# Top-k attention and a leaky-ReLU MLP on one core: the order on ScalarE, scores a slot earlier, a smaller first chunk of tokens and other operations for rounding weights

## The chip, the cores and the metric

The kernel runs on one NeuronCore of a Trainium2 chip. The core has TensorE (PE, matmuls; PEld is its loading of weights), VectorE (DVE), ScalarE (ACT), GpSimd (POOL) and SyncE (SP, which issues the DMAs here). Each has its own instruction queue and works through it in order; semaphores tie them together. The metric is the device time of one execution in microseconds, lower is better.

## What is computed

Attention over 8 batches of 8 heads, 576 tokens and 64 dimensions, in which each query keeps its 32 highest scores, and a two-layer MLP with leaky ReLU on the 4608 tokens of 512 features that come out. All in float32; the MLP's weights arrive as 64-bit floats.

```python
scores = scale * np.matmul(q, k.transpose(0, 1, 3, 2))
kth = np.partition(scores, -top_k, axis=-1)[..., -top_k:-top_k + 1]   # top_k = 32
scores = np.where(scores >= kth, scores, -1000000000.0)
attn = np.exp(scores - np.max(scores, axis=-1, keepdims=True))
attn = attn / (np.sum(attn, axis=-1, keepdims=True) + 1e-09)
x = np.matmul(attn, v)            # then (B,H,S,D) -> (B*S, H*D)
h = x @ w_in                      # 512 -> 2048
out = np.maximum(0.01 * h, h) @ w_out
```

## The kernel before

Heads go in pairs, so that two heads fill 128 partitions of q and k; four pairs make a batch. A *unit* is 128 queries of one pair ("whole") or 64 queries of two pairs ("left", since 576 = 4 x 128 + 64). There are 18 units per batch, 144 in all. A unit is two score tiles of 128 x 576, `u.s[0]` and `u.s[1]`.

The main loop (`for s in ...`, 147 *slots*) is a pipeline written out by hand under `tc.manual_schedule()`: each engine's order is the order of the calls in the loop. In slot s the unit `cur` (s) has its top-k on DVE (`top_k`, L183 and L186: four rounds of two MAX8, three of them with two MATCH_REPLACE8), the unit `old` (s-1) is masked on POOL (`mask`, L195 to L199), `older` (s-2) gets its exponents on ScalarE (`exponents`, L202), its sum plus 1e-9 on POOL (`sums`, L207) and the reciprocal on DVE (`reciprocals`, L211), and `oldest` (s-3, `LAG`) is normalized on ScalarE (`normalize`, L214), transposed on PE with evictions on ScalarE (`transpose_main`, L221 and L223, twice; `transpose_tail`, L228 and L229) and multiplied with the values (`weigh_values`, L251, eviction into the MLP's input `x`, L261). Scores for `new` (s+1) are made on PE and evicted by ScalarE (`scores`, L164 and L173).

The MLP is cut into token chunks, `CHUNKS`. A chunk is ready three slots after its last unit; `slot_budget` spreads its work evenly over the slots until the next chunk is ready, and `mlp_steps` issues that much at each of six places (`SLOTS`) in a slot. A step is two matmuls, of the first pass (L271, tile `ph`, eviction with leaky ReLU L277 into `gT`) or of the second (L282, tile `pz`, eviction L289, store L290). `mlp_cost` counts the work in columns. [...]

In the first slots the weights are turned from 64-bit into 32-bit floats, 32 chunks of 128 x 512 (`convert_weights`, L104 to L114): DVE takes exponent and mantissa bits (L104, L105), POOL clamps the exponent (L106), ScalarE scales both (L107, L108), and in the next call of `convert`, DVE puts them together (L110, L112) and POOL multiplies (L114). Each raw chunk has one of three buffers, and its load (L93) waits for one; a slot calls `convert` three or four times.

## Time and profile before

| | |
|---|---|
| median of 3 runs | 1966.16 us (1962.93 to 1968.38) |
| the profiled execution's own time | 1969.71 us |
| its span, first to last instruction | 1967.9 us |
| PE busy | 1651.5 us, 84% |
| DVE busy | 1498.1 us, 76% |
| POOL busy | 1189.6 us, 60% |
| ScalarE busy | 987.9 us, 50% |

The profile is of one execution. A busy share is the time in which an engine works on some instruction; PE's matmuls overlap and their ends are modelled. An average over the span mixes stages with different limits, so stretches and single slots are read as well. A wait is put down to the instruction that released it.

### The profile page before, as it was taken

Reading aid. Unit: us, or ns where it says so; the run is one execution under the profiler, and the core shown is the slowest. Engines: PE = TensorE matmul, PEld = TensorE weight load, DVE = VectorE, ACT = ScalarE, POOL = GpSimd, SP = SyncE. Lnnn points to the kernel's source line nnn. Section 1 sums busy time; section 2 is a strip of 40 time slices with the busy share of each in tenths; the row PEclk is TensorE's granted clock in tenths of the full one; section 3 lists DMA queues with packets and bytes.
Section 4 is the critical chain, followed back from the end, with each engine's and each line's share of the span. In section 5 each row is a group of like instructions: output and inputs, shape, how many; then the busy total and the mean of one; then the engine's idle time right before and its main releaser. Section 6 shows DMA issues by size and latency. Waiting matters only on the chain.

```text
span 1967.9 us, 25462 instructions
## 1 busy us (share of the span) xinstructions
PE 1651.5 (84%) x8864; PEld 963.6 (49%) x8864; DVE 1498.1 (76%) x3152; ACT 987.9 (50%) x2069; POOL 1189.6 (60%) x934
## 2 busy tenths in 40 slices
PE   2124688889899899898898898898898999899999
PEld 1123556455455455455455455455455455455575
DVE  7888988888887877777787877887787777776700
ACT  2344555565555555555555555555555455555441
POOL 5766766666665666666666665665665666665520
PEclk9956899999999999999999999999999999999999
DMA  4232010001100010000100010000100010000000
GB/s 163 80 110 87 12 54 13 18 6 37 36 18 1 11 54 19 18 6 25 38 28 1 11 54 13 18 12 25 36 30 1 6 36 8 11 11 1 12 6 16
DMA packets 22976, 56.22 MB, mean 29 GB/s; under 512 B 2240, under 2 KB 2240, under 8 KB 22848
## 3 DMA queue, kind: packets, MB, share of 16 engines
q1 hardware_dynamic: 22848, 54.60, 8.3%
q8 instruction: 70, 1.15, 0.2%
q14 instruction: 58, 0.48, 0.1%
HBM read 45.15 MB, written 9.44 MB: 28 GB/s over the span
## 4 chain that ended last, share of the span: by engine, by line
PE 71%; ACT 18%; POOL 4%; issue 3%; DVE 2%; DMA 0%; SPq 0%; POOLq 0%; ACTq 0%
PE pz L282 25%; PE ph L271 18%; PE psc L164 9%; PE po L251 9%; PE main L221 8%; ACT s_sb L214 7%; ACT s_sb L202 4%; ACT wT L223 4%; PE tail L228 2%; ACT s_sb L173 2%; ACT gT L277 1%; POOL pen L197 1%; POOL w_in L114 1%; POOL ex L106 1%; POOL w_out L114 1%
## 5 line engine op out<-in xcount | busy, mean ns | idle before, releaser
L197 POOL TENSOR_SCALAR pen<-s_sb,tops 128x576 f32<-128x576 f32 x288 | 639.5, 2221 | 27.3
L183 DVE MAX8 tops<-rest 128x8 f32<-128x576 f32 x864 | 607.7, 744 | 0.0
L271 PE MATMUL ph<-x,w_in 128*128 128x384 f32 (+2 forms) x1792 | 575.4, 457 | 0.0
L282 PE MATMUL pz<-w_out,gT 128*128 128x512 f32 x1152 | 542.0, 603 | 0.0
L221 PE MATMUL main<-ident,s_sb 128*115 128x128 f32 x1152 | 203.0, 301 | 273.0 <-ACT s_sb L214 271.7
L199 POOL TENSOR_TENSOR s_sb<-s_sb,pen 128x576 f32<-128x576 f32 x288 | 411.9, 1430 | 24.0
L186 DVE MATCH_REPLACE8 rest<-tops,rest 128x576 f32<-128x576 f32 x576 | 423.1, 742 | 0.0
L207 POOL TENSOR_SCALAR ze<-z 128x2 f32<-128x2 f32 x144 | 37.3, 259 | 604.3 <-ACT s_sb L202 604.2
L271 PEld LDWEIGHTS ph<-x,w_in 128*128 128x128 f32 x1792 | 308.1, 196 | 146.9 <-issue 40.4
L221 PEld LDWEIGHTS main<-ident,s_sb 128*115 128x115 f32 x1152 | 156.9, 187 | 399.8 <-ACT s_sb L214 336.0
L211 DVE RECIPROCAL rz<-ze 128x2 f32<-128x2 f32 x144 | 23.7, 165 | 372.8 <-POOL ze L207 372.6
L282 PEld LDWEIGHTS pz<-w_out,gT 128*128 128x128 f32 x1152 | 203.7, 192 | 200.8 <-issue 199.7
L173 ACT COPY s_sb<-psc 128x576 f32<-128x576 f32 x288 | 169.9, 642 | 189.7 <-PE psc L164 189.7
L223 ACT COPY wT<-main 115x512 f32<-115x512 f32 x288 | 168.7, 586 | 156.8 <-PE main L221 155.3
L164 PE MATMUL psc<-kt,qt 64*128 64x288 f32 (+1 forms) x1280 | 203.0, 439 | 38.6 <-ACT s_sb L173 31.2
L214 ACT ACTIVATE s_sb<-s_sb,rz 128x576 f32<-128x576 f32 x288 | 222.9, 774 | 0.0
L202 ACT ACTIVATE s_sb<-s_sb,nbias 128x576 f32<-128x576 f32 x288 | 222.7, 773 | 0.0
L186 DVE MATCH_REPLACE8 rest<-tops,s_sb 128x576 f32<-128x576 f32 x288 | 211.5, 742 | 0.0
L183 DVE MAX8 tops<-s_sb 128x8 f32<-128x576 f32 x288 | 202.0, 742 | 7.3 <-ACT s_sb L173 7.3
L251 PEld LDWEIGHTS po<-wT,vt 115*64 115x64 f32 (+1 forms) x3200 | 162.0, 140 | 88.4 <-issue 82.6
L251 PE MATMUL po<-wT,vt 115*64 115x128 f32 (+3 forms) x3200 | 195.9, 272 | 1.0 <-ACT wT L223 1.0
L164 PEld LDWEIGHTS psc<-kt,qt 64*128 64x128 f32 (+1 forms) x1280 | 110.4, 182 | 108.2 <-issue 45.5
(26 smaller groups left out, 677.9 us busy)
## 6 DMA issues: line engine op xcount, KB each, us to landing
vt<-in_vk_dram SPq DMA_DIRECT2D x32, 290.0 KB
qt<-in_qT_dram SPq DMA_DIRECT2D x32, 288.0 KB
kt<-in_kT_dram SPq DMA_DIRECT2D x32, 288.0 KB
out_dram<-o_sb SPq DMA_DIRECT2D x36, 256.0 KB
raw<-in_moe_w_in_dram SPq DMA_DIRECT2D x16, 512.0 KB
raw<-in_moe_w_out_dram SPq DMA_DIRECT2D x16, 512.0 KB
```

Of the source, the lines that this page charges most:

```text
L164: nc.tensor.matmul(ps[i][r0:r0 + u.rows, half, 0:HS], qt[d, u.q0:u.q0 + u.rows], kt[d, half * HS:(half + 1) * HS], start=True, stop=True,)
L183: nc.vector.max(out=u.tops[:, i, r, :], in_=src[i])
L186: nc.vector.match_replace(out=rest[i], in_to_replace=u.tops[:, i, r, :], in_values=src[i], imm_value=LOWEST)
L197: nc.gpsimd.tensor_scalar(pen, u.s[i], u.tops[:, i, ROUNDS - 1, 7:8], MASKED, ALU.is_lt, ALU.mult)
L199: nc.gpsimd.tensor_tensor(u.s[i], u.s[i], pen, ALU.add)
L202: nc.scalar.activation(u.s[i], u.s[i], AF.Exp, bias=u.nbias[:, i:i + 1], scale=SCALE, accum_out=u.z[:, i:i + 1])
L214: nc.scalar.activation(u.s[i], u.s[i], AF.Copy, bias=0.0, scale=u.rz[:, i:i + 1])
L221: nc.tensor.transpose(main[0:KLEN[c], c, :], u.s[i][:, c * KSTEP:c * KSTEP + KLEN[c]], ident)
L223: nc.scalar.copy(u.wT[0:KSTEP, i, 0:NKC - 1, :], main[0:KSTEP])
L251: nc.tensor.matmul(po[side * D:(side + 1) * D, o, :], vt[0:KLEN[c], c, side, :], u.wT[0:KLEN[c], i, c, r0:r0 + n], start=(c == 0), stop=(c ...
L271: nc.tensor.matmul(ph[:, 0:n], w_in[c][:, f * P:(f + 1) * P], x[c][:, 0:n], start=(c == 0), stop=(c == HP - 1),)
L282: nc.tensor.matmul(pz[:, 0:DMODEL], gT[f][:, i * P:(i + 1) * P], w_out[f // 4][:, f % 4, :], start=(f == 0), stop=(f == NFC - 1),)
```

## The change

On ScalarE both normalizes of `oldest` come first in a slot, and exponents come ahead of the transposes' evictions; the sum plus 1e-9 moves from POOL to ScalarE. Both masks of `old` come first on POOL. `scores` now serves unit s+2 and stands right after `weigh_values`. The MLP is issued at seven places. The chunks of tokens begin with 64 and 128 and end with 192, and in even batches the left units (tokens 0 to 63) come first, in odd ones last. `convert` keeps two chunks in flight and is called four times per slot. The two bit operations on DVE take their constants from a 128 x 1 tile `bits`, read as a repeated column, as second tensor operand; the mantissa and the fraction are kept in the destination instead of a `man` tile and the raw buffer. One value tile, one output tile fewer; q and k are loaded a slot earlier.

The diff, cut to its core (of the loop only what stands there now):

```diff
-    CHUNKS = [128, 256] + [384] * 10 + [256, 128]
+    CHUNKS = [64, 128] + [384] * 11 + [192]
...
-        frac = lo.bitcast(F32)
-        ex = raws.tile([P, WCH], U32, name="ex", bufs=2)
-        man = raws.tile([P, WCH], U32, name="man", bufs=2)
-        nc.vector.tensor_scalar(ex, hi, 20, 0x7FF, ALU.logical_shift_right, ALU.bitwise_and)
-        nc.vector.tensor_scalar(man, hi, 0xFFFFF, None, ALU.bitwise_and)
+        frac, man = lo.bitcast(F32), dst.bitcast(U32)
+        ex = raws.tile([P, WCH], U32, name="ex")
+        nc.vector.scalar_tensor_tensor(out=ex, in0=hi, scalar=20, in1=bits[:, 0:1].to_broadcast([P, WCH]),
+                                       op0=ALU.logical_shift_right, op1=ALU.bitwise_and)
+        nc.vector.tensor_tensor(man, hi, bits[:, 1:2].to_broadcast([P, WCH]), ALU.bitwise_and)
...
-        nc.vector.scalar_tensor_tensor(out=frac, in0=man, scalar=2.0 ** -20, in1=frac,
+        nc.vector.scalar_tensor_tensor(out=dst, in0=man, scalar=2.0 ** -20, in1=frac,
...
-        nc.gpsimd.tensor_tensor(dst, frac, ex.bitcast(F32), ALU.mult)
+        nc.gpsimd.tensor_tensor(dst, dst, ex.bitcast(F32), ALU.mult)
...
+        first = b % 2 == 0
...
-        units += left + whole if b % 2 else whole + left
+        units += left + whole if first else whole + left
...
-        nc.gpsimd.tensor_scalar(u.ze, u.z, 1e-9, None, ALU.add)
+        nc.scalar.activation(u.ze, u.z, AF.Copy, bias=1e-9, scale=1.0)
...
-    SLOTS = 6
+    SLOTS = 7
...
-        finish_conversions()
+        if len(converting) == 2 or not raw_chunks:
+            for c in converting[:1]:
+                next(converting.pop(0), None)
...
             next(picks, None)
             if old:
                 mask(old, 0)
+                mask(old, 1)
+            if oldest:
+                normalize(oldest, 0)
+                normalize(oldest, 1)
+            convert()
+            mlp_steps(budget)
+            if older:
+                exponents(older, 0)
+            if oldest:
+                transpose_main(oldest, 0)
+            mlp_steps(budget)
+            next(picks, None)
+            convert()
+            if older:
+                exponents(older, 1)
+                sums(older)
+            if oldest:
+                transpose_main(oldest, 1)
+            mlp_steps(budget)
+            if oldest:
+                transpose_tail(oldest)
+            next(picks, None)
+            convert()
+            mlp_steps(budget)
+            if older:
+                reciprocals(older)
+            mlp_steps(budget)
+            next(picks, None)
+            if oldest:
+                weigh_values(oldest)
             if new:
                 scores(new)
             convert()
             mlp_steps(budget)
...
             mlp_steps(budget)
             attended(s)
```

How this moves instructions, at three places. ScalarE before, one slot in the middle of the kernel, from the evictions of scores to the eviction of `x` (`s_sb` are score tiles, with numbers; L202 is the exponent, L214 the normalize, L223 and L229 evict transposes):

```order
L173 COPY s_sb_6957<-psc_6951 128x576
L173 COPY s_sb_6959<-psc_6952 128x576
L202 ACTIVATE s_sb_6703,z<-s_sb_6703,nbias 128x576
L214 ACTIVATE s_sb_6615<-s_sb_6615,rz 128x576
L202 ACTIVATE s_sb_6705,z<-s_sb_6705,nbias 128x576
L223 COPY wT<-main 115x512
L214 ACTIVATE s_sb_6617<-s_sb_6617,rz 128x576
L223 COPY wT<-main 115x512
L229 COPY wT<-tail 116x2x128
L289 COPY o_sb<-pz 128x512
L261 COPY x_6054<-po 128x128
```

ScalarE after, a slot of the same kind (L178 evicts scores, L219 normalizes, L207 is the exponent, L212 the sum, L228 and L234 evict transposes):

```order
L178 COPY s_sb_6401<-psc_6395 128x576
L178 COPY s_sb_6403<-psc_6396 128x576
L219 ACTIVATE s_sb_6069<-s_sb_6069,rz 128x576
L219 ACTIVATE s_sb_6071<-s_sb_6071,rz 128x576
L207 ACTIVATE s_sb_6150,z<-s_sb_6150,nbias 128x576
L228 COPY wT<-main 115x512
L207 ACTIVATE s_sb_6152,z<-s_sb_6152,nbias 128x576
L212 ACTIVATE ze<-z 128x2
L228 COPY wT<-main 115x512
L234 COPY wT<-tail 116x2x128
L266 COPY x_5532<-po 128x128
```

The two normalizes moved from behind the exponents, and the second one from behind an eviction of transposes, to right behind the scores' evictions.

PE before, from the transposes of one slot to the scores that stand at the head of the next (L221 and L228 transposes, L282 MLP, L251 values, L164 scores):

```order
L221 MATMUL main<-ident,s_sb_6615 115x128 x4
L221 MATMUL main<-ident,s_sb_6617 115x128 x4
L282 MATMUL pz<-w_out_94,gT_107 128x512
L282 MATMUL pz<-w_out_94,gT_108 128x512
L228 MATMUL tail<-ident,s_sb_6615 116x128
L228 MATMUL tail<-ident,s_sb_6617 116x128
L282 MATMUL pz<-w_out_94,gT_109 128x512
L282 MATMUL pz<-w_out_94,gT_110 128x512
L251 MATMUL po<-wT,vt 64x128 x10
L164 MATMUL psc_7037<-kt,qt 128x288
L164 MATMUL psc_7038<-kt,qt 128x288
L164 MATMUL psc_7037<-kt,qt 128x288
```

PE after, the same piece of a slot (L226 and L233 transposes, L288 MLP, L256 values, L169 scores):

```order
L226 MATMUL main<-ident,s_sb_5986 115x128 x4
L226 MATMUL main<-ident,s_sb_5988 115x128 x4
L288 MATMUL pz<-w_out_94,gT_100 128x512
L288 MATMUL pz<-w_out_94,gT_101 128x512
L233 MATMUL tail<-ident,s_sb_5986 116x128
L233 MATMUL tail<-ident,s_sb_5988 116x128
L288 MATMUL pz<-w_out_95,gT_102 128x512
L288 MATMUL pz<-w_out_95,gT_103 128x512
L256 MATMUL po<-wT,vt 64x128 x10
L169 MATMUL psc_6395<-kt,qt 128x288
L169 MATMUL psc_6396<-kt,qt 128x288
L169 MATMUL psc_6395<-kt,qt 128x288
```

Nothing moved on PE here: the scores stand behind the value products in both, at the end of a slot instead of the head of the next.

DVE before, in the first unit, two calls of `convert` with a round of top-k between them:

```order
L110 SCALAR_TENSOR_TENSOR raw<-man,raw 128x512
L112 SCALAR_TENSOR_TENSOR ex<-raw,ex 128x512
L104 TENSOR_SCALAR ex<-raw 128x512
L105 TENSOR_SCALAR man<-raw 128x512
L183 MAX tops<-rest_156 128x8
L183 MAX tops<-rest_157 128x8
L186 MATCH_REPLACE rest_156<-tops,rest_156 128x576
L186 MATCH_REPLACE rest_157<-tops,rest_157 128x576
L110 SCALAR_TENSOR_TENSOR raw<-man,raw 128x512
L112 SCALAR_TENSOR_TENSOR ex<-raw,ex 128x512
```

DVE after, the calls at the same place:

```order
L114 SCALAR_TENSOR_TENSOR w_in_90<-w_in_90,raw 128x512
L116 SCALAR_TENSOR_TENSOR ex<-raw,ex 128x512
L107 SCALAR_TENSOR_TENSOR ex<-raw,bits 128x512
L109 TENSOR_TENSOR w_in_92<-raw,bits 128x512
L188 MAX tops<-rest_167 128x8
L188 MAX tops<-rest_168 128x8
L114 SCALAR_TENSOR_TENSOR w_in_91<-w_in_91,raw 128x512
L116 SCALAR_TENSOR_TENSOR ex<-raw,ex 128x512
L107 SCALAR_TENSOR_TENSOR ex<-raw,bits 128x512
L109 TENSOR_TENSOR w_in_93<-raw,bits 128x512
```

Each call finishes the chunk that was begun two calls earlier (`w_in_90`, then `w_in_91`) instead of the one before, and L105's tile `man` is gone.

## Rows read from the trace of the kernel before

**Rows 1.** engines' busy time and share of the span, instructions (the page)

```profile
PE 1651.5 (84%) x8864; PEld 963.6 (49%) x8864; DVE 1498.1 (76%) x3152; ACT 987.9 (50%) x2069; POOL 1189.6 (60%) x934
```

**Rows 2.** busy time of each engine (and instructions) in two stretches; then granted clock, DMA share, GB/s

```profile
413.30:1755.50 1342.20, 1214.49 (x6456) 681.39 (x6456) 1059.87 (x2273) 710.74 (x1479) 835.27 (x650) 0.99 0.06 21
1755.50:1967.90 212.40, 208.43 (x1006) 128.17 (x1002) 83.07 (x180) 85.05 (x187) 74.51 (x59) 1.00 0.03 9
```

**Rows 3.** the same view, of the reciprocals L211 alone, in three stretches

```profile
68.60:205.80 137.20, 0.91 (x6) 0.68 0.28 94
219.70:248.80 29.10, 0.44 (x3) 0.97 0.01 1
418.25:1760.70 1342.45, 17.92 (x108) 0.99 0.06 21
```

**Rows 4.** timeline of PE: start, us, what; in brackets idle time before, its releaser

```profile
1100.16 0.69 PE L221 MATMUL main<-ident,s_sb 128*115 128x128 f32 x4 [1.35 <-ACT s_sb L214]
...
1106.86 3.70 PE L282 MATMUL pz<-w_out,gT 128*128 128x512 f32 x8
1110.39 0.60 PE L221 MATMUL main<-ident,s_sb 128*115 128x128 f32 x4
1112.34 0.69 PE L221 MATMUL main<-ident,s_sb 128*115 128x128 f32 x4 [1.35 <-ACT s_sb L214]
```

**Rows 5.** timeline of ScalarE in the same slot

```profile
1107.01 1.18 ACT L173 COPY s_sb<-psc 128x576 f32<-128x576 f32 x2 [0.94 <-PE psc L164]
...
1108.85 0.77 ACT L214 ACTIVATE s_sb<-s_sb,rz 128x576 f32<-128x576 f32 x1
1109.51 0.77 ACT L202 ACTIVATE s_sb<-s_sb,nbias 128x576 f32<-128x576 f32 x1
...
1111.03 0.59 ACT L223 COPY wT<-main 115x512 f32<-115x512 f32 x1 [0.66 <-PE main L221]
1111.51 0.78 ACT L214 ACTIVATE s_sb<-s_sb,rz 128x576 f32<-128x576 f32 x1
```

**Rows 6.** waits, slots 27 to 134: us in total, times, longest

```profile
PE main L221 <- ACT s_sb L214: 126.6, 125, 1.4
```

**Rows 7.** groups by line, the conversion's four on DVE: busy us, mean ns

```profile
L105 DVE TENSOR_SCALAR man<-raw 128x512 uint32<-128x512 uint32 x32 | 33.2, 1037 | 0.0
L110 DVE SCALAR_TENSOR_TENSOR raw<-man,raw 128x512 f32<-128x512 uint32 x32 | 28.7, 898 | 0.1
...
L112 DVE SCALAR_TENSOR_TENSOR ex<-raw,ex 128x512 uint32<-128x512 uint32 x32 | 21.9, 683 | 24.0 <-ACT ex L108 24.0
...
L104 DVE TENSOR_SCALAR ex<-raw 128x512 uint32<-128x512 uint32 x32 | 13.6, 425 | 4.4 <-DMA raw<-in_moe_w_in_dram 4.4
```

**Rows 8.** timeline of DVE and GpSimd, at two places of the conversion

```profile
61.78 1.40 POOL L199 TENSOR_TENSOR s_sb<-s_sb,pen 128x576 f32<-128x576 f32 x1
62.00 1.73 DVE L110 SCALAR_TENSOR_TENSOR raw<-man,raw 128x512 f32<-128x512 uint32 x1
...
98.65 0.41 DVE L104 TENSOR_SCALAR ex<-raw 128x512 uint32<-128x512 uint32 x1
98.80 1.41 POOL L114 TENSOR_TENSOR w_in<-raw,ex 128x512 f32<-128x512 f32 x1 [1.23 <-DVE ex L112]
98.98 1.51 DVE L105 TENSOR_SCALAR man<-raw 128x512 uint32<-128x512 uint32 x1
```

**Rows 9.** timeline of DVE and ScalarE at the start

```profile
7.30 1.42 DVE L183 MAX8 tops<-s_sb 128x8 f32<-128x576 f32 x2 [7.30 <-ACT s_sb L173]
...
11.96 1.18 ACT L173 COPY s_sb<-psc 128x576 f32<-128x576 f32 x2 [4.15 <-PE psc L164]
```

**Rows 10.** weight loads: DMA rate in 4 us; issue on SP; the wait for it

```profile
100.00:104.00 4.00, 0.89 (x4) 0.89 (x4) 4.00 (x9) 3.00 (x7) 0.99 (x3) 0.61 0.35 131
...
22.63 11.21 SPq L93 DMA_DIRECT2D raw<-in_moe_w_in_dram  x3
...
35.37 0.43 DVE L104 TENSOR_SCALAR ex<-raw 128x512 uint32<-128x512 uint32 x1 [4.39 <-DMA raw<-in_moe_w_in_dram]
```

More of the change, by code (lines that the diff above doesn't have):

```diff
@@ L150 @@
     for b in range(B):
[L151 removed]
+        first = b % 2 == 0
+        whole = [Unit(b, [b * HP + hp], q0 + LEFT * first)
                  for q0 in range(0, S - LEFT, P) for hp in range(HP)]
[L153 removed]
+        left = [Unit(b, [b * HP + hp, b * HP + hp + 1], 0 if first else S - LEFT)
                 for hp in range(0, HP, 2)]
[L155 removed]
+        units += left + whole if first else whole + left
     def scores(u):
@@ L278, in mlp @@
             yield 2 * max(n, 225)
-        for i in range(n // P):
+        for r0 in range(0, n, P):
+            m = min(P, n - r0)
             pz = ps_ml.tile([P, 512], F32, name="pz", tag="ml")
@@ L365 @@
         last = {p: n for n, u in enumerate(units) for p in u.pairs}
-        load_qk(0)
-        scores(units[0])
-        fetch_weights()
-        for p in range(1, HP):
+        for p in range(HP):
             load_qk(p)
-            fetch_weights()
-        for p in range(HP):
-            load_v(p)
+            if p % 2:
+                scores(units[p // 2])
+            if p < 3:
+                fetch_weights()
         def load_more(s):
-            for of, load, lag in ((qk_of, load_qk, -1), (v_of, load_v, LAG)):
-                while len(of) < NPAIR and (len(of) < LOADED or last[len(of) - LOADED] + lag <= s):
+            for of, load, n, lag in ((qk_of, load_qk, LOADED, -2), (v_of, load_v, LOADED_V, LAG)):
+                while len(of) < NPAIR and (len(of) < n or last[len(of) - n] + lag <= s):
                     load(len(of))
         for s in range(len(units) + LAG):
-            cur, new, old = unit(s), unit(s + 1), unit(s - 1)
-            older, oldest = unit(s - 2), unit(s - LAG)
+            cur, old = unit(s), unit(s - 1)
+            older, oldest, new = unit(s - 2), unit(s - LAG), unit(s + 2)
             picks = top_k(cur) if cur else iter(())
@@ L389 @@
                 mask(old, 0)
-            if new:
-                scores(new)
+                mask(old, 1)
+            if oldest:
+                normalize(oldest, 0)
+                normalize(oldest, 1)
             convert()
```

45 lines of the change are left out of this document (16 added, 29 removed).

## The prediction, made before the changed kernel ran

> **What bounds the kernel now.** I read the busy shares first [rows 1], then the stretches [rows 2], then the period of the loop, taken from the one reciprocal that each slot issues [rows 3], then one slot on PE and ScalarE [rows 4, 5] and the waits [rows 6]. "Slot" is one pass of the loop over units, s = 0 to 146.
>
> PE is the fullest engine, yet only 84% busy, and VectorE (DVE) comes second with 76% [rows 1]. The shares hide three stages. While weights are converted, six slots took 137.2 us, 22.9 us each; DVE sets that pace. Behind it three slots took 29.1 us, 9.70 each, with DVE still the pace: that is what one slot's top-k costs it. From slot 27 to 134, 108 slots took 1342.4 us, 12.43 each [rows 3]. There DVE is busy for 1059.9 of 1342 us and PE for 1214.5 [rows 2], so neither is full: a wait sets the period. PE's wait for ScalarE's normalize (L214) comes to 126.6 us in that stretch, 1.17 per slot [rows 6]. Rows 4 and 5 show why. In this slot PE runs its MLP steps to 1110.39, then the first transposes; the second ones start only at 1112.34, 1.35 us after PE went idle. On ScalarE the second normalize starts at 1111.51, because ahead of it in the queue stand two score evictions, two exponents and the eviction of the first transposes. DVE's idle 282 us there are the echo: it has nothing to do until the slot moves on. After slot 134 more MLP work is handed to each slot and PE is full (208.4 of 212.4 us [rows 2]).
>
> **The change, part by part.**
>
> *ScalarE's order (slots 21 to 140).* PE's own order in these slots does not change: scores of unit s+2 at the end of slot s are the same place as before at the start of slot s+1. So the gain must come from ScalarE. Now both normalizes stand directly behind the score evictions. From the end of PE's scores: evictions 1.18, two normalizes at about 0.67 from start to start [rows 5] make 2.5 us. PE meanwhile has four MLP matmuls, 3.53 us [rows 4], then the first transposes, so neither pair of transposes waits. In slots of the first MLP pass an MLP eviction (at most the 0.59 us of the eviction in rows 5) can stand ahead, and PE's cover is four to six matmuls of 384 columns, 2.6 to 4 us at 1.72 ns a column (below); it still holds, but by 0.1 or 0.2 us in one slot of three. What is late next: the exponents and then the sum, now on ScalarE (144 instructions on two elements; at a third of a normalize's 0.77 us, an estimate, 37 us on an engine that is 53% busy here [rows 2]). DVE's reciprocal waits for that sum, and behind it stand only the last round of that unit and the next unit. DVE needs 9.70 of a longer slot, and the normalize that needs the reciprocal comes half a slot later. GpSimd loses the sum, and with it a wait on ScalarE in front of its mask; the mask has a slot in hand. So I take the whole wait away: 12.43 - 1.17 = 11.26 us a slot. Bounds: 11.0 (the slot of rows 4, 12.18 from one second transposes to the next, would be 10.83 without the gap), and 11.85 if half of the wait comes back.
>
> *Rounding of weights (slots 0 to 8).* Before, a chunk costs DVE L104, L105, L110, L112: 0.425 + 1.037 + 0.898 + 0.683 = 3.04 us [rows 7], about 2.74 from start to start. Undisturbed they cost 0.33, 0.33, 0.60, 0.60 = 1.86, so 0.88 per chunk is blocking: L105 takes 1.51 when GpSimd's multiply slips in, L110 takes 1.73 beside GpSimd's add [rows 8]. The new L107 and L109 read two operands and can't be faster than L110's 0.60, so the free cost rises to 2.40. Whether they block is not in the trace, since no operand there is a repeated column. Ends: 2.40 (nothing blocks) and 4.55 (each chunk pays both of the worst cases, 1.1 and 1.05). I take 2.40 + 0.88 = 3.28, as L110, the nearest row, is blocked too.
>
> The Trainium skill (SBUF — State Buffer, Who interferes with whom) says that a VectorE instruction with two SBUF inputs contends with a GpSimd instruction that reads SBUF. L110's rows agree; by that rule the new forms escape nothing, and the value near 3.28 or above holds; with forms that escape it the sum would be 28 us lower.
>
> Two chunks are now in flight, so the 24.0 us in which DVE's L112 waited for ScalarE's exponent [rows 7] go; I take 0 left. The raw buffer is now free when DVE has read it, not after GpSimd's multiply, but the load that takes it is needed at the next conversion call instead of the one after. The gap is two of the new operations, a round of top-k and two more: 1.2 + 2.8 + 1.2 = 5.2 us, where the round is a third of 9.70 less the short last one of 1.4 [rows 9]; across that short one it is 3.8. A load alone was through in 4 us (131 GB/s x 4 us = 524 KB [rows 10]), so I price it at nothing.
>
> *64-token first chunk, left units first.* The first unit needs two pairs of q and k: its scores wait for the second pair, whose evictions ran at 11.96. DVE starts near 12.6 instead of 7.30 [rows 9], 5.3 us lost. The MLP then has chunks ready at slots 4, 8, 20, 32 ... 140, 146 (before 6, 14, 26 ... 134, 142, 146). By the code's own cost (64 x max(n, 225) + blocks of 128 x 8192 columns) the whole MLP grows from 602,240 to 616,640 columns. One column costs 3.53 us / 2048 = 1.72 ns [rows 4], so PE gets 25 us more, but half-empty slots 5 to 20 hide the small first chunk.
>
> **The sum**, against the profiled execution (span 1967.9, own time 1969.7).
> - Slots 0 to 8: 12.6 + 8 x (9.70 + 4 x 3.28) - 2.4 (the first two calls finish nothing) + 12.1 (slot 8: top-k and two finishing halves) = 204.9. Before, this point was near 210.
> - Slots 9 to 20: 128 tokens of MLP over 12 slots, 1,883 columns or 3.2 us each; with 3.8 us of attention (10.83 less eight MLP matmuls of 0.88) PE needs 7.0 us, less than DVE's 9.70. 12 x 9.70 = 116.4, to 321. PE enters slot 21 about 3 us sooner, at 318.
> - Slots 21 to 140: 120 x 11.26 = 1351, to 1669.
> - The end: before, 104,640 columns from slot 135 on are 180 of 212.4 us, so 32 us are attention of 12 slots. Now 79,936 columns are 137.5, and six slots of attention with two left units 18: 155.5, to 1825.
> Add 1.8 us around the span: 1827. The profiled execution lies 3.6 us above the median of the runs, so 1823. The gain, some 143 us, is mostly 108 waits (127); faster first slots give most of the rest.
>
> **Rivals.**
> - *Half of the wait re-forms.* For: the cover is thin in some slots, and the exponents and two evictions of transposes now stand between the sum and DVE. Against: the chain above has slack in the slot of rows 4 and 5. 120 x 0.59 = +70: 1893.
> - *The new forms block nothing.* 32 x 0.88 = -28: 1795.
> - *PE falls to the lower clock in slots 9 to 20.* It is idle there for 2.7 of 9.7 us. In the conversion slots, where PE had little to do, the granted clock averaged 0.68, a mix of 1.2 and 2.4 GHz; in the three slots at 9.70 us it was 0.97 [rows 3], with much the same PE load as I expect, which speaks against it. At 1.2 GHz PE needs up to 14.0 us a slot: 12 x 4.3 = +52: 1875. The Trainium skill (TensorE: Matmul & The Clock Gate, HAM oscillation) holds that idle gaps between bursts throttle PE again; the 0.97 row doesn't bear it out at this load.
> - *Slower: loads of weights set the pace of the first slots.* The load issued at 22.63, with v behind and beside it, was what DVE waited for until 35.37 [rows 10], 12.7 us. If each of 29 loads took that against a gap of 5.2, DVE would lose 7.5 x 29 = 218: 2041. It decides from 4.9 us per load (143 / 29). Against: v loads now come one per slot, not four in a row.
>
> **How the numbers follow.** Forecast 0.60; half of the wait 0.18; forms free 0.09; lower clock 0.06; loads 0.06; 0.01 for no change (within 0.3%, about what a measurement here can tell). All but the last two are faster: 0.93 faster, 0.01 same, 0.06 slower. The likeliest case gives 1823; its own range is 1785 (11.0 us slots) to 1860. The range to hold 8 in 10 goes to the rival on either side: 1785 to 1893.
>
> **What would show it.** PE's wait for the normalize in the long stretch falls from 126.6 to under 20 us; the reciprocals come 11.0 to 11.4 us apart; DVE waits for the sum on ScalarE, about 1 us a slot; L109 averages 1 us or more (0.6 would be the free form); the last conversion ends near 205; PE is about 91% busy. I am wrong if reciprocals stay 12 us apart, or if DVE waits for weight loads in the first 200 us.

## The result, and the profile after

The changed kernel takes 1770.29 us, median of four runs (1769.01 to 1771.27), against 1964.55 us (1962.37 to 1968.38) for the kernel before, run beside it: a ratio of 0.9009, interval 0.8992 to 0.9026. It is faster, by 194 us where 143 were forecast, and the time lies below the range, whose lower end was 1785. The profiled execution took 1769.01 us with a span of 1767.2.

The page's line of engines, answering to [rows 1]:

```profile
PE 1620.1 (92%) x8896; PEld 972.1 (55%) x8896; DVE 1498.9 (85%) x3154; ACT 993.5 (56%) x2214; POOL 1175.8 (67%) x790
```

Four stretches, as in [rows 2]: start and end, length, busy time of PE, its weight loads (PEld), DVE, ScalarE and GpSimd, then granted clock, DMA share, GB/s. The first is the conversion of weights, the second runs to the value products of slot 20, the third holds slots 27 to 134, the fourth is what follows the start of the value products of slot 140:

```profile
15.00:205.10 190.10, 78.98 (x418) 59.53 (x414) 171.79 (x301) 78.13 (x169) 153.23 (x102) 0.78 0.29 95
205.10:321.40 116.30, 92.84 (x632) 63.07 (x630) 116.01 (x252) 73.92 (x175) 91.63 (x62) 0.93 0.10 30
384.60:1546.30 1161.70, 1161.16 (x6457) 682.04 (x6456) 1056.86 (x2270) 713.77 (x1587) 808.79 (x541) 1.00 0.07 24
1609.60:1767.20 157.60, 153.68 (x693) 89.96 (x692) 28.84 (x64) 45.96 (x106) 28.32 (x19) 1.00 0.03 10
```

In the third, PE is busy for 1161.2 of 1161.7 us; before, it was 1214.5 of 1342.2 [rows 2], for the same matmuls (6,456, one more in the second window). So 127 us of idle time went, and some 53 us of what had been shown as busy. The reciprocals (L216, L211 before), as in [rows 3], give the slot's period. The first line holds seven slots (its x8 counts both ends), the conversion and what directly follows it; the second twelve slots behind that; the third the 108 long slots:

```profile
72.80:217.90 145.10, 1.04 (x8) 0.71 0.28 92
217.90:334.30 116.40, 1.81 (x12) 0.93 0.11 34
403.90:1565.60 1161.70, 17.78 (x108) 1.00 0.07 24
```

That is 9.70 us a slot in the second and 10.76 in the third, where before took 12.43. In the first line, the five slots from 72.8 to 191.8 us take 23.8 us each, more than the 22.9 of before [rows 3]; that DVE still ends its last conversion sooner (205.1 us against 214.3) comes from four chunks in every slot, where before has three or four. One slot on PE, then on ScalarE, answering to [rows 4, 5] (L276 and L282 are the hidden layer and its eviction, L226 the transposes, L178 the score evictions, L219 the normalizes). A matmul of the scores, the MLP or the value products stands as two records in these traces, so that x8 is four matmuls of the code; a transpose stands as one:

```profile
1106.72 1.24 PE L169 MATMUL psc<-kt,qt 64*128 64x288 f32 x8
1107.89 2.85 PE L276 MATMUL ph<-x,w_in 128*128 128x384 f32 x8
1110.58 0.60 PE L226 MATMUL main<-ident,s_sb 128*115 128x128 f32 x4
1111.02 1.46 PE L276 MATMUL ph<-x,w_in 128*128 128x384 f32 x4
1112.31 0.60 PE L226 MATMUL main<-ident,s_sb 128*115 128x128 f32 x4
```

```profile
1107.99 1.18 ACT L178 COPY s_sb<-psc 128x576 f32<-128x576 f32 x2 [0.89 <-PE psc L169]
1109.06 1.45 ACT L219 ACTIVATE s_sb<-s_sb,rz 128x576 f32<-128x576 f32 x2
1110.78 0.49 ACT L282 ACTIVATE gT<-ph 128x384 f32<-128x384 f32 x1 [0.27 <-PE ph L276]
1111.17 0.77 ACT L207 ACTIVATE s_sb<-s_sb,nbias 128x576 f32<-128x576 f32 x1
```

The two normalizes run from 1109.06 to 1110.51. The first transposes, which need only the first of them, start at 1110.58, and no PE row has a bracket of idle time. The matmuls' row has no wait for the normalize left in these 108 slots; the weight loads' row has 22.7 us:

```profile
PEld main L226 <- ACT s_sb L219: 22.7, 45, 0.7
```

### The profile page after: what moved, and what is told of

Read it like the earlier page. It is cut to its first block, busy times and chain, and to the rows that moved or that the text cites. A ratio compares the mean times of both kernels' runs of the same rounds, so it can differ in the third digit from the quotient of the medians.

```text
span 1767.2 us, 25274 instructions
## 1 busy us (share of the span) xinstructions
PE 1620.1 (92%) x8896; PEld 972.1 (55%) x8896; DVE 1498.9 (85%) x3154; ACT 993.5 (56%) x2214; POOL 1175.8 (67%) x790
## 4 chain that ended last, share of the span: by engine, by line
PE 83%; DVE 9%; POOL 6%; ACT 1%; issue 1%; DMA 0%; SPq 0%; POOLq 0%; ACTq 0%
PE pz L288 29%; PE ph L276 27%; PE po L256 9%; PE psc L169 9%; PE main L226 7%; DVE tops L188 4%; DVE rest L191 3%; POOL s_sb L204 2%; POOL pen L202 2%; PE tail L233 2%; POOL w_in L118 1%; POOL ex L110 1%; ACT s_sb L219 1%; DVE ex L107 0%; ACT o_sb L295 0%
## 5 line engine op out<-in xcount | busy, mean ns | idle before, releaser
L202 POOL TENSOR_SCALAR pen<-s_sb,tops 128x576 f32<-128x576 f32 x288 | 638.3, 2216 | 403.7 <-DVE tops L188 190.7
L276 PE MATMUL ph<-x,w_in 128*128 128x384 f32 (+3 forms) x1792 | 567.0, 458 | 23.6 <-ACT gT L282 23.4
L288 PE MATMUL pz<-w_out,gT 128*128 128x512 f32 (+1 forms) x1184 | 554.7, 602 | 0.0
L204 POOL TENSOR_TENSOR s_sb<-s_sb,pen 128x576 f32<-128x576 f32 x288 | 421.1, 1462 | 24.0
L276 PEld LDWEIGHTS ph<-x,w_in 128*128 128x128 f32 x1792 | 315.8, 199 | 186.5 <-issue 34.1
L288 PEld LDWEIGHTS pz<-w_out,gT 128*128 128x128 f32 (+1 forms) x1184 | 206.4, 188 | 213.3 <-issue 209.1
L178 ACT COPY s_sb<-psc 128x576 f32<-128x576 f32 x288 | 169.9, 642 | 150.2 <-PE psc L169 150.2
L169 PE MATMUL psc<-kt,qt 64*128 64x288 f32 (+1 forms) x1280 | 206.2, 443 | 38.4 <-ACT s_sb L178 31.5
L226 PEld LDWEIGHTS main<-ident,s_sb 128*115 128x115 f32 x1152 | 156.5, 184 | 128.3 <-ACT s_sb L219 59.3
L207 ACT ACTIVATE s_sb<-s_sb,nbias 128x576 f32<-128x576 f32 x288 | 222.1, 771 | 0.0
L226 PE MATMUL main<-ident,s_sb 128*115 128x128 f32 x1152 | 172.0, 285 | 49.9 <-ACT s_sb L219 49.4
L256 PEld LDWEIGHTS po<-wT,vt 115*64 115x64 f32 (+1 forms) x3200 | 162.7, 141 | 96.3 <-issue 85.6
L219 ACT ACTIVATE s_sb<-s_sb,rz 128x576 f32<-128x576 f32 x288 | 207.4, 772 | 8.5 <-DVE rz L216 8.5
L266 ACT COPY x<-po 128x128 f32<-128x128 f32 (+1 forms) x160 | 39.4, 256 | 292.6 <-PE po L256 292.5
L256 PE MATMUL po<-wT,vt 115*64 115x128 f32 (+3 forms) x3200 | 196.6, 272 | 7.2 <-ACT wT L228 7.2
L228 ACT COPY wT<-main 115x512 f32<-115x512 f32 x288 | 164.4, 571 | 28.4 <-PE main L226 28.4
L169 PEld LDWEIGHTS psc<-kt,qt 64*128 64x128 f32 (+1 forms) x1280 | 111.1, 183 | 90.8 <-ACT s_sb L178 35.3
L282 ACT ACTIVATE gT<-ph 128x384 f32<-128x384 f32 (+3 forms) x224 | 99.7, 446 | 103.6 <-PE ph L276 103.6
```

Source lines behind the costliest of these rows:

```text
L169: nc.tensor.matmul(ps[i][r0:r0 + u.rows, half, 0:HS], qt[d, u.q0:u.q0 + u.rows], kt[d, half * HS:(half + 1) * HS], start=True, stop=True,)
L178: nc.scalar.copy(s_sb.rearrange("p (h n) -> p h n", h=2), ps[i][:, :, 0:HS])
L202: nc.gpsimd.tensor_scalar(pen, u.s[i], u.tops[:, i, ROUNDS - 1, 7:8], MASKED, ALU.is_lt, ALU.mult)
L204: nc.gpsimd.tensor_tensor(u.s[i], u.s[i], pen, ALU.add)
L207: nc.scalar.activation(u.s[i], u.s[i], AF.Exp, bias=u.nbias[:, i:i + 1], scale=SCALE, accum_out=u.z[:, i:i + 1])
L219: nc.scalar.activation(u.s[i], u.s[i], AF.Copy, bias=0.0, scale=u.rz[:, i:i + 1])
```

## The experiments

Each was timed beside the kernel before on the same chip (medians there 1960.7, 1964.2 and 1964.6 us, so that some 4 us between kernels of different groups can be the chip). "Full change" is the kernel after. The slot period is taken from the start of the value products of slot 26 to that of slot 134, 108 slots; before has 12.43 by this mark and the full change 10.76.

| kernel | median us | ratio to before, interval | slot, us |
|---|---|---|---|
| before, both normalizes moved (e1) | 1761.82 | 0.8973, 0.8941 to 0.9005 | 10.81 |
| before, second half's moved (e9) | 1843.90 | 0.9396, 0.9374 to 0.9418 | 11.35 |
| before, first half's moved (e11) | 1939.70 | 0.9873, 0.9853 to 0.9892 | 12.16 |
| full change, normalizes back among the exponents (e5) | 2124.49 | 1.0831, 1.0788 to 1.0874 | 13.49 |
| full change, normalizes and main transposes back in their places (e6) | 1916.76 | 0.9763, 0.9730 to 0.9796 | 11.85 |
| full change, old rounding forms (e2) | 1755.54 | 0.8941, 0.8903 to 0.8979 | 10.76 |
| full change, old chunks and unit order (e3) | 1750.24 | 0.8916, 0.8885 to 0.8947 | 10.76 |
| both of these (e7) | 1734.61 | 0.8835, 0.8806 to 0.8863 | 10.76 |
| e7, four exponent buffers (e10) | 1731.33 | 0.8817, 0.8783 to 0.8851 | 10.76 |
| e7, one conversion in flight (e8) | 1755.05 | 0.8939, 0.8910 to 0.8968 | 10.76 |
| e7, sums on GpSimd (e4b) | 1737.16 | 0.8845, 0.8830 to 0.8860 | 10.76 |
| e7, scores one ahead, at the slot's head (e12) | 1837.22 | 0.9346, 0.9324 to 0.9368 | 11.53 |

### The normalizes alone

```diff
             if new:
                 scores(new)
+            if oldest:
+                normalize(oldest, 0)
+                normalize(oldest, 1)
             convert()
...
                 exponents(older, 0)
-            if oldest:
-                normalize(oldest, 0)
-            if older:
                 exponents(older, 1)
...
                 transpose_main(oldest, 0)
-                normalize(oldest, 1)
```

> The kernel before, with nothing changed but the two normalizes, which now stand right behind the evictions of scores on ScalarE. Theory A (this order is nearly the whole gain, and the wait it removes is the one that the weight load of the transposes shows, 197.3 us in slots 27 to 134, 1.83 a slot, not the 126.6 us that the matmuls show): the slots from 26 to 134 fall from 12.43 to 10.6 to 10.8 us, the total to 1750 to 1780. Theory B (the order is worth the 1.17 us a slot of the matmuls' row, and the other half microsecond comes from scores two units ahead, seven places for the MLP and the sum on ScalarE): 11.2 to 11.3 us a slot, a total near 1830.

Measured: 1761.82 us, 8 us below the full change itself. Moving two instructions a slot gives nearly the whole of the steady gain, 1.62 of 1.67 us a slot. The same 108 slots of before and then of e1, columns as above:

```profile
412.00:1754.50 1342.50, 1214.79 (x6458) 681.50 (x6457) 1060.17 (x2273) 710.74 (x1479) 835.47 (x651) 0.99 0.06 21
```

```profile
380.70:1548.00 1167.30, 1165.91 (x6459) 677.43 (x6458) 1063.44 (x2283) 688.80 (x1479) 835.40 (x650) 1.00 0.07 24
```

The stretch shrank by 175.2 us. Only 126.3 of that is idle time of PE; 48.9 came out of its busy time, with the number of matmuls unchanged. Groups of PE in that stretch, of before and then of e1 (busy us, mean ns, idle before them) show where:

```profile
L271 PE MATMUL ph<-x,w_in 128*128 128x384 f32 x1152 | 429.1, 504 | 0.0
...
L221 PE MATMUL main<-ident,s_sb 128*115 128x128 f32 x864 | 146.3, 292 | 127.7 <-ACT s_sb L214 126.6
```

```profile
L271 PE MATMUL ph<-x,w_in 128*128 128x384 f32 x1152 | 419.5, 494 | 0.0
...
L221 PE MATMUL main<-ident,s_sb 128*115 128x128 f32 x864 | 118.0, 273 | 0.0
```

The same transposes are shown 28.3 us longer where they wait; the hidden layer is 9.6 us longer in the stretch with a granted clock of 0.99 instead of 1.00; the other 11 us are overlap between groups. So busy time holds part of the price of a wait, and the idle column is not the whole of it. The starts say the same: in before, the second transposes start 0.05 us after the second normalize ends in all 108 slots, and the idle column has a wait at only 89 of them.

### One normalize at a time

```diff
 e9_second_only (against the kernel before)
                 scores(new)
+            if oldest:
+                normalize(oldest, 1)
...
                 transpose_main(oldest, 0)
-                normalize(oldest, 1)
```

```diff
 e11_first_only (against the kernel before)
                 scores(new)
+            if oldest:
+                normalize(oldest, 0)
...
                 exponents(older, 0)
-            if oldest:
-                normalize(oldest, 0)
-            if older:
                 exponents(older, 1)
```

> Kernel before with one edit: the normalize of the second half moves up right behind the scores, the one of the first half stays between the exponents. In the trace of before TensorE waits 102.2 us in slots 26 to 134 for the second half's (it is queued behind the eviction of the first half's transposes, which TensorE must make first) and 25.5 us for the first half's. Theory A (each wait can be taken away alone, in proportion to what the trace shows): four fifths of the gain of moving both, slots of about 11.1 us, 1785 to 1815 us. Rival (the loop from the first transposes over their eviction to the second normalize is all that holds the slot, and the first half's wait goes with it): 1755 to 1775 us, as with both moved.

> Kernel before with one edit: the normalize of the first half moves up right behind the scores, the one of the second half stays behind the first half's transposes. Theory A (each wait can be taken away alone, in proportion): a fifth of the gain of moving both, slots of about 12.1 us, 1905 to 1940 us. Rival (the second half's normalize still has to wait for the first half's transposes, and what the first wait gives the second takes): 1950 us or more, no change.

Measured: 1843.90 and 1939.70 us, gains of 121 and 25 us where moving both gives 199 on its chip. e11 is at the edge of what proportion gave, e9 29 us beyond it; neither rival held. The two gains come to 146, so the waits are not independent. PE's waits in the 108 slots, of e9 and then of e11 (us, times, longest):

```profile
PE main L221 <- ACT s_sb L214: 48.1, 54, 1.0
```

```profile
PE main L221 <- ACT s_sb L214: 123.6, 108, 1.8
```

Split by which pair of transposes was idle, before has 25.5 us (36 times) at the first and 102.2 (89 times) at the second. Without the second's wait the first's grows to 48.1 (54 times); without the first's, the second's comes in every slot and grows to 123.6. A wait that ends earlier only brings PE to the next one sooner, so the gain of both is more than the gains of each.

### The old places in the full change

e5 put the normalizes between and behind the exponents and the transposes directly behind; e6 also put back the MLP stretch that the kernel before has between the exponents and the first transposes.

```diff
 e5_order_back (against the full change)
-            if oldest:
-                normalize(oldest, 0)
-                normalize(oldest, 1)
             convert()
             mlp_steps(budget)
             if older:
                 exponents(older, 0)
             if oldest:
+                normalize(oldest, 0)
+            if older:
+                exponents(older, 1)
+                sums(older)
+            if oldest:
                 transpose_main(oldest, 0)
+                normalize(oldest, 1)
```

```diff
 e6_old_places (against e5_order_back)
                 sums(older)
+            mlp_steps(budget)
+            next(picks, None)
+            convert()
             if oldest:
                 transpose_main(oldest, 0)
                 normalize(oldest, 1)
             mlp_steps(budget)
-            next(picks, None)
-            convert()
             if oldest:
                 transpose_main(oldest, 1)
-            mlp_steps(budget)
-            if oldest:
                 transpose_tail(oldest)
```

> The changed kernel with the normalizes back where they stood: the first between the two exponents, the second behind the eviction of the first transposes; all else as changed. Theory A: the slots go back to 12.2 us or more and the total to 1930 to 1960. Theory B: 11.9 us a slot, a total near 1910, since the other parts keep their half microsecond.

> Full change with the steps of the weights put back where the kernel before had them: first-half exponent, first-half normalize, second-half exponent, sums, then an MLP stretch, then the transposes with the second normalize between them. The stretch is what the earlier kernel with the order put back (2124 us) had lost: there the transposes stood directly behind the exponents. Theory A (the places of the normalizes are the whole of the steady gain; 2124 us came from the missing MLP stretch between the normalize and the transposes that wait for it): slots 26 to 134 take 12.2 to 12.6 us as in the kernel before, the weight loads of the transposes wait about 1.8 us a slot for the first normalize, and the time is 1930 to 1985 us. Rival B (what makes 2124 is another part of the change, scores at the slot's end or both masks first, which turn against a late normalize): slots stay at 13 us or more and the time is above 2030 us.

Measured: 2124.49 and 1916.76 us. e5 was missed by both theories, since it was no clean undo: with no call of the MLP planner between the first normalize and its transposes, PE waits 185 times in the 108 slots, 106.5 us at the second pair (102.2 in the kernel before) and 95.1 at the first (25.5). In one slot looked at, ScalarE comes to the exponents and the normalize only behind an MLP eviction that PE releases at 1103.19, and the first transposes start at 1105.26. e6 restores the stretch and with it 208 us, so rival B is out. Its slot of 11.85 is still shorter than theory A's 12.2, and in 90 of the 108 slots (37 in the kernel before) four records of MLP matmuls have come to stand between the two pairs of transposes too: PE's idle time at the second pair is 33.1 us, at the first 58.2. So the rest of the change takes 0.58 us off a slot where the normalizes are late (12.43 to 11.85) and 0.05 where they are early (10.81 to 10.76). The 108 slots of e5 and of e6:

```profile
422.70:1880.00 1457.30, 1255.75 (x6457) 706.64 (x6456) 1058.01 (x2269) 726.77 (x1587) 808.31 (x541) 0.96 0.06 19
```

```profile
409.70:1690.00 1280.30, 1189.04 (x6457) 680.91 (x6456) 1057.93 (x2269) 717.37 (x1587) 807.53 (x541) 1.00 0.06 22
```

### Scores one unit ahead

```diff
 e12_scores_one_ahead (against e7; ahead of the loop, the scores of one unit and not of two)
-            older, oldest, new = unit(s - 2), unit(s - LAG), unit(s + 2)
+            older, oldest, new = unit(s - 2), unit(s - LAG), unit(s + 1)
...
                 mask(old, 1)
+            if new:
+                scores(new)
             if oldest:
                 normalize(oldest, 0)
...
                 weigh_values(oldest)
-            if new:
-                scores(new)
```

> As e7_old_chunks_old_forms (1734.6 us) with the scores one unit ahead and at the slot's head, as in the kernel before, the normalizes behind them. Theory A (scores two ahead and beside the value products give nothing in the steady slots, 10.76 there against 10.81 with only the normalizes moved): slots 26 to 134 of 10.7 to 10.9 us, 1730 to 1745 us. Rival (one ahead, the picks wait for the scores' evictions behind ScalarE's queue in the slots that VectorE bounds): slots 8 to 20 above 10 us and 1750 us or more.

Measured: 1837.22 us, 102.6 more than e7, with slots of 11.53. Theory A is wrong. The rival had the side right and the place wrong. VectorE is not held in the slots that it bounds: its top-k of unit 9 and of unit 20 start 106.7 us apart in e12 and in e7, 9.70 a slot (only PE's value products drift there, 10.00 us a slot from slot 8 to 20). It is the 108 long slots that lose, 0.77 each. PE and then ScalarE of e12 in one slot (L225 transposes, L177 score evictions, L218 normalizes):

```profile
1105.55 1.56 PE L275 MATMUL ph<-x,w_in 128*128 128x384 f32 x4
1107.04 1.24 PE L168 MATMUL psc<-kt,qt 64*128 64x288 f32 x8
1108.21 1.56 PE L275 MATMUL ph<-x,w_in 128*128 128x384 f32 x4
1110.21 0.69 PE L225 MATMUL main<-ident,s_sb 128*115 128x128 f32 x4 [0.45 <-ACT s_sb L218]
```

```profile
1108.31 1.18 ACT L177 COPY s_sb<-psc 128x576 f32<-128x576 f32 x2 [2.38 <-PE psc L168]
1109.38 1.45 ACT L218 ACTIVATE s_sb<-s_sb,rz 128x576 f32<-128x576 f32 x2
```

ScalarE does the same work in the same order as in the full change, but fewer MLP matmuls cover it on PE. Between the scores and the first transposes e12 has four records of them in all 108 slots, the full change eight in 90 slots and twelve in 18: three calls of the MLP planner lie between the two in the full change, one here. In e1 the scores are one unit ahead too and nothing is lost; there two calls lie between, and the trace has eight records in all 108 slots. In e12 the first transposes start 0.05 us after the first normalize ends in every one of the 108 slots, while the idle column has a wait at 54. No run changed the number of covering matmuls alone. The 108 slots of e12:

```profile
365.00:1610.70 1245.70, 1220.09 (x6456) 668.85 (x6456) 1059.82 (x2271) 706.67 (x1588) 808.48 (x541) 1.00 0.07 23
```

It is 84.0 us longer than the full change's, and only 25.6 of it is idle time. Not all of the 84.0 is the wait: in e12 MLP matmuls also stand between the value products and the scores (the line at 1105.55). By the starts of PE's matmuls, the way from the value products to the last MLP matmul ahead of the transposes is 0.20 us longer in e12 than in e7 in each of the 108 slots, with the same matmuls on it. That is 21 us by this estimate, and leaves 63 for the wait. The same split stands in 36 of the 108 slots of before and of e1 and in none of the full change, so that the change did move something on PE; 36 times 0.20 is 7 us, near the 5.6 by which e1's stretch is longer than the full change's.

### What a wait costs, over all these runs

Loss is the length of the 108 slots over the 1161.7 us of the full change. "Matmuls" is PE's idle time for the normalize, "weight loads" the same wait read from the weight loads' row.

| kernel | loss | matmuls | weight loads | clock |
|---|---|---|---|---|
| e12 | 84.0 | 24.4 | 115.7 | 1.00 |
| e9 | 64.0 | 48.1 | 113.9 | 1.00 |
| e6 | 118.6 | 91.3 | 189.2 | 1.00 |
| e11 | 151.6 | 123.6 | 160.5 | 1.00 |
| before | 180.8 | 126.6 | 197.3 | 0.99 |
| e5 | 295.6 | 201.5 | 292.2 | 0.96 |

The loss is more than the matmuls' row in every one and, except where the clock was at 0.96, less than the weight loads' row. The first starts to count only at the end that the record gives to the last matmul; the second counts also loads that could have been early while matmuls still ran. Of e12's loss, 21 us are the split and not the wait. Before, e9 and e11 have e1's order on PE; over e1's 1167.3 us they lose 175.2, 58.4 and 146.0, which lies between the two rows as well.

### Rounding forms and chunks

```diff
 e2_old_bit_forms
-        nc.vector.scalar_tensor_tensor(out=ex, in0=hi, scalar=20, in1=bits[:, 0:1].to_broadcast([P, WCH]),
-                                       op0=ALU.logical_shift_right, op1=ALU.bitwise_and)
-        nc.vector.tensor_tensor(man, hi, bits[:, 1:2].to_broadcast([P, WCH]), ALU.bitwise_and)
+        nc.vector.tensor_scalar(ex, hi, 20, 0x7FF, ALU.logical_shift_right, ALU.bitwise_and)
+        nc.vector.tensor_scalar(man, hi, 0xFFFFF, None, ALU.bitwise_and)
```

```diff
 e3_old_chunks
-    CHUNKS = [64, 128] + [384] * 11 + [192]
+    CHUNKS = [128, 256] + [384] * 10 + [256, 128]
...
-        first = b % 2 == 0
+        first = b % 2 == 1
...
-            if p % 2:
-                scores(units[p // 2])
+            if p < 2:
+                scores(units[p])
```

> The changed kernel with the two bit operations of the conversion as tensor_scalar with constants again (two chunks in flight and the destination as scratch stay). Theory A (the new forms only cost: 0.27 us each, and are blocked by GpSimd's multiply just as the old ones): the last conversion ends near 188 instead of 205 us and the total falls by about 17 us. Theory B (the old forms are blocked more, so the new ones pay): conversion ends at 205 or later, the total is the same or up to 15 us longer.

> The changed kernel with the chunks of tokens and the order of units of before (128, 256, 10 x 384, 256, 128; left units last in even batches). Theory A (the small chunk costs 25 us of TensorE and buys less): slots stay DVE's at 9.7 us until slot 26, the total is 10 to 20 us shorter than the changed kernel's. Theory B (earlier MLP work pays): 10 to 25 us longer.

> Full change with the chunks and the unit order of before and with the single-input rounding forms of before. Theory A (the two parts cost 20 and 15 us in different stretches, the end and the first 205 us, and so add up): 1735 us, 1731 to 1740. Rival (both act on the start of the MLP, and the later one hides the earlier): 1745 to 1751 us.

Measured: 1755.54, 1750.24 and 1734.61 us. Both parts only cost, 15 and 20 us, and they add up, as theory A had it each time. The groups on DVE in the conversion (busy us, mean ns), of the full change and then of e2:

```profile
L107 DVE SCALAR_TENSOR_TENSOR ex<-raw,bits 128x512 uint32<-128x512 uint32 x32 | 21.9, 684 | 18.3 <-POOL w_in L118 10.0 <-POOL w_out L118 7.5 <-POOL ex L110 0.5
...
L109 DVE TENSOR_TENSOR w_out<-raw,bits 128x512 uint32<-128x512 uint32 x16 | 16.8, 1051 | 0.0
L109 DVE TENSOR_TENSOR w_in<-raw,bits 128x512 uint32<-128x512 uint32 x16 | 16.4, 1027 | 0.0
```

```profile
L107 DVE TENSOR_SCALAR ex<-raw 128x512 uint32<-128x512 uint32 x32 | 16.7, 523 | 20.1 <-POOL w_in L117 10.0 <-POOL w_out L117 7.5 <-DMA raw<-in_moe_w_in_dram 2.5
...
L108 DVE TENSOR_SCALAR w_out<-raw 128x512 uint32<-128x512 uint32 x16 | 12.6, 789 | 0.0
...
L108 DVE TENSOR_SCALAR w_in<-raw 128x512 uint32<-128x512 uint32 x16 | 7.9, 495 | 0.0
```

Two operations cost 55.1 us in the new forms and 37.2 in the old: 18 us of DVE, of which 15 reach the end. With the old chunks, slot 20's value products start 6 us sooner (315.4 against 321.4), slot 140's 9 us later, and what is left from there is 27 us shorter (130.2 against 157.6). Of the 6 us, 4.8 are VectorE's earlier start: its first top-k begins at 7.65 us and not at 11.92, that of unit 20 at 311.5 and not at 316.3. Behind slot 140 come chunks of 256 and 128 tokens, in the full change of 384 and 192:

```profile
1618.60:1748.80 130.20, 126.39 (x625) 82.01 (x624) 28.87 (x64) 42.94 (x103) 28.37 (x19) 1.00 0.03 11
```

### Conversions in flight, buffers, and the sums

```diff
 e8_one_in_flight (against e7)
-        if len(converting) == 2 or not raw_chunks:
+        if True:
             for c in converting[:1]:
```

```diff
 e10_ex_four (against e7)
-        ex = raws.tile([P, WCH], U32, name="ex")
+        ex = raws.tile([P, WCH], U32, name="ex", bufs=4)
```

```diff
 e4b_sums_gpsimd (against e7)
-        nc.scalar.activation(u.ze, u.z, AF.Copy, bias=1e-9, scale=1.0)
+        nc.gpsimd.tensor_scalar(u.ze, u.z, 1e-9, None, ALU.add)
```

> As e7_old_chunks_old_forms, but with one conversion in flight: each conversion is finished before the next is begun, as in the kernel before. Theory A (two in flight gained nothing: the wait on ScalarE's half of the conversion that it removes, some 2.5 us a slot, has come back as the wait for the exponent buffer, 2.5 us a slot): within 6 us of e7_old_chunks_old_forms. Rival (two in flight hides ScalarE's latency in each of the 32 conversions, about 0.6 us or more each): slower by 15 us or more.

> As e7_old_chunks_old_forms with four buffers instead of three for the exponent words of a conversion, nothing else. In the conversion stage VectorE waits 2.5 us once a slot for GpSimd's last multiply of the conversion three back, 17.5 us in seven slots. Theory A (that wait is the buffer's alone): it goes, slots 2 to 6 take about 19.2 us instead of 21.8, and the time is 15 to 18 us under e7_old_chunks_old_forms. Rival (GpSimd, the raw words' buffers or the next step's input end the same wait a little later): less than 6 us.

> As e7_old_chunks_old_forms (1734.6 us) with the sum's small addition on GpSimd instead of ScalarE, as in the kernel before. Theory A (VectorE's wait for it has slack in the steady slots, and its place there is not on the path): within 4 us of 1734.6. Rival (on GpSimd it queues behind a mask of 2.2 and 1.4 us and holds VectorE in the slots that VectorE bounds, 8 to 20): slower by 8 us or more.

Measured: 1755.05, 1731.33 and 1737.16 us, to be held against e7's 1734.61. One conversion in flight costs 20.4 us: theory A was wrong, two in flight do pay. In e8 the conversion's last DVE operation waits 33.4 us for ScalarE, where e7 waits 20.6 in all, and a slot takes 24.4 us instead of 21.8:

```profile
DVE ex L115 <- ACT ex L111: 33.4, 15, 4.3
```

The fourth buffer gave 3.3 us of the 17.5 that were waited for it, so its rival held, but for another reason than the rival named. The wait is gone; the operations became longer. DVE's groups in the same stretch of e7 and then of e10:

```profile
L115 DVE SCALAR_TENSOR_TENSOR ex<-raw,ex 128x512 uint32<-128x512 uint32 x16 | 10.9, 678 | 0.0
...
L108 DVE TENSOR_SCALAR w_in<-raw 128x512 uint32<-128x512 uint32 x6 | 2.9, 483 | 0.0
```

```profile
L115 DVE SCALAR_TENSOR_TENSOR ex<-raw,ex 128x512 uint32<-128x512 uint32 x17 | 14.9, 878 | 0.6 <-ACT ex L111 0.6
...
L108 DVE TENSOR_SCALAR w_in<-raw 128x512 uint32<-128x512 uint32 x6 | 6.8, 1128 | 0.0
```

DVE's busy time rose from 19.1 to 21.1 us a slot. While DVE waited, GpSimd's multiply ran alone; now DVE runs beside it, and its operations take longer: L115 takes 0.68 us as before, but 1.52 to 1.74 in the seven of 32 places where the multiply had begun ahead of it. The sums cost nothing that can be told: 2.6 us, with the intervals of the two ratios overlapping. By the start of VectorE's top-k of unit 9 (191.3 us against 188.7) all of it is there; from then on both take 9.70 us a slot.

e10 is the fastest kernel seen, 1731.33 us, 39 below the full change: the new order and two conversions in flight, with the old chunks and forms.

## Why the prediction was right and wrong

The direction, the place and the mechanism held. Of the four terms of the sum, three came out within 4 us and one missed by 63.

- **Slots 0 to 8**: forecast to end at 204.9, the last conversion ended at 205.1. That it fits to 0.2 us is luck, as two errors cancel. DVE's idle time was set to nothing, yet L107 waits 18.3 us, nearly all of it for GpSimd's multiply, which must free the exponent buffer. On the other side a chunk's four operations were priced too high: they come to 3.15 us, about 2.85 from start to start (less the 0.30 that the prediction took off before's 3.04 for overlap), not 3.28, which is 14 us over 32 chunks; and DVE started at 11.9, not 12.6. The remaining 4 us or so are not accounted for.
- **L109** averages 1.03 to 1.05 us where the prediction had 0.60 for a two-input operation that nothing blocks, so the new forms are blocked too: the rival that blocks nothing is out, as "1 us or more" foretold. The Trainium skill (SBUF — State Buffer, Who interferes with whom) has two-input VectorE instructions contend with a GpSimd instruction that reads SBUF; the trace agrees: where GpSimd's multiply had the start, L109 takes up to 1.76 us, and where L109 runs at its 0.68 beside it, the multiply stretches (2.26 us in the one at 95.52, 1.41 in [rows 8]). That the repeated column is what counts as the second input is not shown by it, since L105 with one input was held to 1.51 too [rows 8].
- **Slots 9 to 20**: 9.70 us a slot, as forecast; the granted clock averaged 0.93 there, and the rival of the lower clock is out.
- **The end**: 155.5 forecast, 157.6 from the value products of slot 140 on.
- **Slots 21 to 140** is the step that failed. It said "So I take the whole wait away: 12.43 - 1.17 = 11.26 us a slot", 1351 us in all; the stretch took 1288.2, from 321.4 to 1609.6, 10.73 a slot. The wait did go whole, and nothing took its place. But 1.17 was PE's idle time for the normalize [rows 6], and removing the same wait alone (e1) took 1.62 us off a slot, the full change 1.67. PE's busy time of 11.25 a slot [rows 2] was taken as work, and it was not all work: 0.45 to 0.50 of it went with the wait (some 0.09 of that with the clock, the hidden layer's 9.6 us). The weight loads' row of before had the wait at 197.3 us, 1.83 a slot:

```profile
PEld main L221 <- ACT s_sb L214: 197.3, 162, 1.6
```

The truth lies between these two readings, and the prediction took the lower one as its value. It had a better one in hand as a bound: the slot of [rows 4] without its gap, 12.18 - 1.35 = 10.83. The range stopped at 11.0 and so left out 10.76 (11.0 in its own sum gives 1792, not the 1785 that it names; 10.83 gives 1771, which would have been right in part by luck, as it comes from one slot). The Trainium skill (Perfetto Trace Analysis, Tensor Engine Instruction) says that a matmul's end in the profile is estimated from its size and a delay and not observed. No run here can test that; what the traces show is that the same transposes average 292 ns where they wait and 273 where they do not.

- **Half of the wait re-forms**: it did not, but the cover is as thin as was said, and in more slots: in 45 of the 108 the weight loads wait for the normalize (22.7 us), and the first transposes start 0.05 to 0.36 us after it ends, where 0.1 or 0.2 us in one slot of three was forecast. In the slot shown there are some 0.7 us. e12, with half the cover, loses 0.77 us a slot, of which 0.20 are the split.
- **"PE's own order in these slots does not change"**: true of 72 of the 108 slots; in 36 the kernel before had MLP matmuls between the value products and the scores.
- **Two in flight**: the 24.0 us went, and two in flight are worth 20.4 us (e8), but "I take 0 left" missed the 18.3 us for the exponent buffer that came in their place.
- **The sum on ScalarE**: DVE waits for it 104.8 us in the 108 slots of the full change, 1.0 a slot, "about 1 us" as forecast. That this costs nothing there is what e4b shows: 10.76 us a slot with the sum on either engine.
- **Chunks**: the sum's own pieces held, and so did "half-empty slots 5 to 20 hide the small first chunk": slots 9 to 20 keep DVE's 9.70 us. What going back to the old chunks gains, 20 us (18.4 between the profiled executions), is for the most part VectorE's earlier start (4.8, where the prediction had priced 5.3) and a shorter way from slot 20 to the end: 27.4 us less behind the start of slot 140's value products, 15.0 more before it. The prediction never asked what the part was worth alone, and so did not see that two parts of the change cost 35 us together.
- **Loads of weights set the pace**: they did not; DVE waits 0.3 us for them in the full change, and at most 3.0 in the variants with two in flight.

## What to carry to other kernels

A wait on PE costs more than PE's idle row shows: estimate the new period by that of a repeated slot less its gap (10.83 here, 10.76 measured), and keep the matmuls' and the weight loads' readings as the two ends. In an in-order queue it is worth asking which two or three instructions another engine waits for; moving these two did nearly all that a rewritten order did, and moving one at a time let the other wait grow. Price each part of a bundled change alone, since parts that only cost hide well under one large gain. When work on PE is to cover a wait elsewhere, count the matmuls between the two in the trace: with four records between scores and transposes they waited in every slot, with eight in e1 in none.

## What the runs showed of the hardware

- PE's busy time is not a measure of work: with all matmuls kept, it fell by 48.9 us (e1) when they no longer waited; e12's stretch was 84.0 us longer than the full change's and showed 25.6 as idle; 21 (an estimate) were the split.
- Removing 17.5 us of buffer waits on DVE returned 3.3 us, because its operations then overlap GpSimd's multiply: the same operation went from 678 to 878 ns on average, one with a single input from SBUF and a constant (L108) from 483 to 1128.
- An operation of VectorE and one of GpSimd held each other up in pairs of some forms and not of others: L109 took 0.68 to 1.76 us beside GpSimd's multiply, and the multiply up to 2.26, while GpSimd's L202 (2.2 us, one tensor and a scalar per partition) and VectorE's L114 (two tensors) ran together 16 times in the full change's conversion at 2.21 to 2.22 and 0.67 to 0.68 us.
- The granted clock fell in some of the kernels that wait, and not in others: over the 108 slots it averaged 0.96 in e5 (201.5 us of idle time for the normalize) and 0.99 in the kernel before (126.6), almost all of it the 2.4 GHz level with short stretches at 1.2, but 1.00 in e11 with 123.6, as in e1 with none. Where it fell, what the waits cost includes that.
